# The rounded half of a gelu result copied by GpSimd instead of ScalarE, with a later due time for the half that follows

## The chip, the cores and the metric

The kernel runs on one core of a Trainium2 chip. A core has a matrix engine (TensorE, "PE" in the profile; its weight loads are shown apart as "PEld"), VectorE ("DVE"), ScalarE ("ACT"), GpSimd ("POOL") and SyncE ("SP"), which here only issues DMAs. Every engine works through its own list of instructions strictly in order, and waits for the others through semaphores. Operands lie in SBUF, results of matmuls in PSUM. The metric is the time of one execution on the device, in microseconds (us); less is better.

## What is computed

For 2048 rows x of width 512 the reference mixes two branches, a windowed attention with 32 heads of width 16 and a dense network with a gelu, by a sigmoid gate of each row:

```python
qkv = (x @ wqkv)                        # 32 heads of 16
scores = (q @ k.T) * 16 ** -0.5         # each row sees itself and the 255 rows before it
a = softmax(masked scores) @ v @ wo
h = gelu(x @ w1 + b1)                   # tanh form, width 1792
b = h @ w2 + b2
g = sigmoid((x * gate_w).sum(-1))
out = g * a + (1 - g) * b
```

Everything is float32. TensorE is given float32 numbers rounded to a shorter form ("fp32r"), so the kernel splits each operand of the dense products into a high half (the number rounded to fp32r) and a low half (the number minus its high half), and makes each product out of three matmuls: high by high, high by low, low by high.

## The kernel before

**Tiling.** Rows are worked in 4 blocks of 512. The dense work is one long stream: the qkv projection of the four blocks, then eight dense stages (four row blocks, each with the first and with the second half of the 1792 hidden columns), then the output projection. Each dense stage has a first part, "u", which makes 7 tiles of 128 hidden columns (12 matmuls each: 4 slices of the inner width, three matmuls each, lines 109 to 111), each followed by the gelu; and a second part, "y", which multiplies the 7 gelu results h with w2, for four groups of 128 rows.

**Attention runs in between.** While TensorE works through the dense stages, the main loop slips attention matmuls between the dense ones: line 522 makes a score tile of which VectorE takes row maxima (line 526); line 566 makes another score tile, of which ScalarE takes the exponential into a tile named pt (line 588); GpSimd zeroes the masked corners of pt (line 582, four instructions for a finished block) and copies the maxima into the operand of line 566 (line 548, "put", eight small copies per 512 rows); line 610 multiplies pt with v ("PV"). Each kind of score tile has three PSUM buffers. The last blocks of attention are masked by VectorE instead of GpSimd.

**Order.** The order of instructions on all engines is written out by the program. A counter in nanoseconds advances with each matmul that is issued; `after(ns, fn)` puts a piece of work into a heap with a due time, and it is appended to its engine's list when the counter passes that time. `need(key)` issues pending work until a key is done. So a due time is no wait: it only decides between which other instructions of its engine a piece of work stands. The waits come from data and from buffers being reused.

**The gelu** is function `gelu`, called 100 ns after the last matmul of a u tile. It has seven steps for each 128x512 tile: line 721 on ScalarE writes x1 = u + b1 into an SBUF buffer; f1 (line 724, ScalarE) squares u + b1 in PSUM; f2 (727, VectorE) forms the argument of tanh in sq; f3 (730, ScalarE) takes tanh; f4 (733, VectorE) makes x1 = (tanh + 1) * x1, which is twice the gelu; f5 (736) writes the high half h[:, 0], a copy that rounds to fp32r; f6 (739, VectorE) writes the low half h[:, 1] = x1 - h[:, 0] and marks h as issued. The tuple GELU holds the due times of f1 to f6 after the first step. The buffer tag "x1" has two buffers, so the line 721 of a tile waits until f6 of the tile two before it has read x1. Tag "sq" has two buffers as well, h has seven.

In part y the tiles of h are used in the order 0 to 5 for the first 128 rows, 0 to 2 for the second 128 rows, then tile 6 for the first rows (constant YSWAP = 3), and so on. Of the three matmuls of such a product the first two (lines 109 and 110) read the high half of h, and the third (line 111) reads the low half and waits for f6.

**Other work of the same engines** in the dense stages: weights are split like the activations, the high half by ScalarE (line 179), the low half by VectorE or, early on, in turn by GpSimd (line 183); line 631 (ScalarE) and 634 (VectorE) evacuate PV; line 814 (VectorE) evacuates y.

Of the kernel before, what the change touches and what calls it, by code (L numbers as in the profile page):

```python
# [12 lines left out]
AF = mybir.ActivationFunctionType  # L13
# [19 lines left out]
def gated_mix(ctx: ExitStack, tc: tile.TileContext, x, wqkv, wo, w1, b1, w2, b2, gate_w, out):  # L33
    nc = tc.nc
# [11 lines left out]
    def f32(ap):  # L46
        return ap.bitcast(F32)
# [68 lines left out]
    def after(ns, fn, *args):  # L116
        now[1] += 1
        heapq.heappush(todo, (now[0] + ns, now[1], fn, args))
# [598 lines left out]
    def gelu(p, f, h):  # L717

        x1 = sb.tile([128, T], F32, tag="x1", bufs=2, name=f"x1{h.name}")
        sq = sb.tile([128, T], F32, tag="sq", bufs=2, name=f"sq{h.name}")  # L720
        nc.scalar.activation(x1, p, AF.Identity, bias=b1c[:, f:f + 1])

        def f1():
            nc.scalar.activation(p, p, AF.Square, bias=b1c[:, f:f + 1])

        def f2():
            nc.vector.scalar_tensor_tensor(sq, p, GC, x1, op0=ALU.add, op1=ALU.mult)  # L727

        def f3():
            nc.scalar.activation(sq, sq, AF.Tanh, scale=GS)  # L730

        def f4():
            nc.vector.scalar_tensor_tensor(x1, sq, 1.0, x1, op0=ALU.add, op1=ALU.mult)

        def f5():
            nc.scalar.activation(h[:, 0], x1, AF.Copy)

        def f6():
            nc.vector.tensor_sub(h[:, 1], x1, f32(h[:, 0]))
            done.add(h.name)  # L740
        for ns, fn in zip(GELU, (f1, f2, f3, f4, f5, f6)):
            after(ns, fn)
# [258 lines left out]
START = 105000.0  # L1001
NORM = 6000
YSWAP = 3
GELU = (700, 1500, 3600, 4600, 6000, 7000)
XAT = 3
ORDER = 'mspf'
XOR = 1
# [38 lines left out]
```

## Time and profile before

| quantity | value |
|---|---|
| time, median of 3 runs (lowest, highest) | 742.09 us (740.79, 743.92) |
| time of the profiled execution | 741.31 us |
| its span, first to last instruction | 739.5 us |
| granted TensorE clock, share of full speed | 0.999 |
| VectorE busy | 516.3 us (70%) |
| ScalarE busy | 420.3 us (57%) |
| DMA queues' share of 16 engines, main queue | 82.6% |
| f6, line 739 (56 times) | 41.3 us, mean 738 ns |
| f4, line 733 (56 times) | 41.6 us, mean 743 ns |
| select, line 582 (538 times) | 217.7 us, mean 425 ns |

The profile is of one execution. A line such as "L736 ACT ACTIVATE h<-x1h" names the line of the kernel, the engine, the operation, and the tile written and read. A timeline row gives start and duration in us; where it ends in brackets, these hold the time that the engine sat idle before and what ended it. Matmuls are pipelined: a row of a matmul lasts about 0.39 us for 512 columns while the next one starts 0.23 us later, so that the starts tell the rate, and busy time of TensorE says little.

### The profile page before, as it was taken

The numbers are of one execution on the slowest core, as the hardware profiler recorded it, in microseconds if no ns is written. First come the engines' busy times: TensorE is split into PE (matmuls) and PEld (weight loads), VectorE is DVE, ScalarE is ACT, GpSimd is POOL, SyncE is SP. The second block draws the span as 40 slices with busy tenths as digits, with TensorE's granted clock in tenths as the row PEclk, the third lists the DMA queues.
The fourth block names the chain that finished last, engine by engine and source line by source line (L and its number), as shares of the span: only waits on it lengthen the run. The fifth ranks groups of instructions, "written<-read, shape, count | busy, mean of one in ns | idle before, by whom it ended". The sixth has DMA issues, their size and how long they took to land.

```text
span 739.5 us, 17486 instructions
## 1 busy us (share of the span) xinstructions
PE 729.2 (99%) x6129; PEld 603.7 (82%) x6129; DVE 516.3 (70%) x1567; ACT 420.3 (57%) x972; POOL 360.1 (49%) x846
## 2 busy tenths in 40 slices
PE   8999999999999999999999999999999999999998
PEld 7888888887788888888888887888888888877786
DVE  3632326789768867986798699767867886774552
ACT  4434532358537844863695479447735853795551
POOL 4200000339656765776587668757765775630000
PEclk9999999999999999999999999999999999999999
DMA  9989798999995687799676999996798799568672
GB/s 313 340 270 408 254 398 270 257 328 197 294 243 143 159 246 199 179 226 269 156 187 160 241 214 239 261 244 150 178 268 241 185 228 253 137 185 230 204 242 112
DMA packets 179255, 172.09 MB, mean 233 GB/s; under 512 B 56672, under 2 KB 122976, under 8 KB 179168
## 3 DMA queue, kind: packets, MB, share of 16 engines
q1 hardware_dynamic: 179168, 170.97, 82.6%
q8 instruction: 49, 0.80, 0.5%
q14 instruction: 38, 0.31, 0.2%
HBM read 108.53 MB, written 62.39 MB: 231 GB/s over the span
## 4 chain that ended last, share of the span: by engine, by line
PE 85%; DVE 5%; ACT 4%; DMA 4%; issue 2%; POOL 0%; SPq 0%; POOLq 0%; DVEq 0%; ACTq 0%
PE sm L522 9%; PE st L566 8%; PE pv_sm L610 7%; PE y L109 7%; PE y L111 7%; PE y L110 7%; PE u L109 5%; PE u L110 5%; PE u L111 5%; PE qk L109 4%; PE qk L111 4%; PE qk L110 4%; PE a L109 2%; PE v L109 2%; PE v L111 2%; PE v L110 2%
## 5 line engine op out<-in xcount | busy, mean ns | idle before, releaser
L526 DVE CUSTOM_DVE_ANT_0 sm<-sm,mask 128x320 f32<-128x320 f32 (+4 forms) x512 | 234.0, 484 | 87.1 <-PE sm L522 81.3
L588 ACT ACTIVATE pt<-st 128x320 f32<-128x320 f32 (+4 forms) x512 | 199.9, 426 | 138.1 <-PE st L566 135.0
L582 POOL TENSOR_SCALAR_AFFINE_SELECT pt<-pt 64x256 f32<-64x256 f32 (+1 forms) x538 | 217.7, 425 | 118.7 <-ACT pt L588 108.7
L522 PE MATMUL sm<-kd,qd 96*128 96x320 f32 (+4 forms) x512 | 152.9, 310 | 2.8 <-DVE M L526 2.7
L566 PE MATMUL st<-qs,ks 128*128 128x320 f32 (+4 forms) x512 | 153.7, 309 | 0.8 <-ACT pt L588 0.8
L548 POOL CAST qs<-tt 4x256 fp32r<-4x256 f32 x256 | 121.5, 475 | 47.7 <-DVE tt L541 33.3
L522 PEld LDWEIGHTS sm<-kd,qd 96*128 96x128 f32 x512 | 96.4, 188 | 26.1 <-DVE M L526 6.4
L566 PEld LDWEIGHTS st<-qs,ks 128*128 128x128 f32 x512 | 97.1, 190 | 18.1 <-ACT pt L588 2.2
L109 PE MATMUL y<-w,h 128*128 128x512 f32 x224 | 88.6, 396 | 0.6 <-DVE sqh L727 0.6
L111 PE MATMUL y<-w,h 128*128 128x512 f32 x224 | 87.9, 392 | 0.0
L110 PE MATMUL y<-w,h 128*128 128x512 f32 x224 | 87.8, 392 | 0.0
L109 PE MATMUL u<-mx,w 128*128 128x512 f32 x196 | 79.9, 408 | 0.0
L110 PE MATMUL u<-mx,w 128*128 128x512 f32 x196 | 77.3, 395 | 0.0
L111 PE MATMUL u<-mx,w 128*128 128x512 f32 x196 | 77.1, 393 | 0.0
L610 PE MATMUL pv_sm<-pt,vbuf 64*32 64x320 f32 (+4 forms) x1408 | 73.0, 346 | 0.0
L610 PE MATMUL pv_st<-pt,vbuf 64*32 64x320 f32 (+4 forms) x1408 | 72.6, 346 | 0.0
L526 DVE DVE_READ_ACCUMULATOR2_ANT M<- 128x1 f32 x512 | 71.6, 140 | 0.0
L610 PEld LDWEIGHTS pv_sm<-pt,vbuf 64*32 64x32 f32 x1408 | 48.9, 106 | 20.7 <-issue 1.7
L326 DVE TENSOR_TENSOR qke<-qk,qke 128x512 fp32r<-128x512 f32 x32 | 22.1, 689 | 46.2 <-ACT qke L323 30.4
L323 ACT ACTIVATE qke<-qk 128x512 fp32r<-128x512 f32 x32 | 19.1, 598 | 55.4 <-PE qk L111 32.9
L111 PEld LDWEIGHTS y<-w,h 128*128 128x128 f32 x224 | 42.0, 188 | 9.8
L109 PEld LDWEIGHTS y<-w,h 128*128 128x128 f32 x224 | 42.4, 189 | 4.5 <-DVE sqh L727 0.9
(148 smaller groups left out, 1288.6 us busy)
## 6 DMA issues: line engine op xcount, KB each, us to landing
kd<-SK SPq DMA_DIRECT2D x32, 384.0 KB
qs<-SQ SPq DMA_DIRECT2D x64, 192.0 KB
mx<-XT SPq DMA_DIRECT2D x24, 512.0 KB
SQ<-qke SPq DMA_DIRECT2D x16, 512.0 KB
SK<-qke SPq DMA_DIRECT2D x16, 512.0 KB
ND<-nd SPq DMA_DIRECT2D x32, 256.0 KB
raw_w<-in_B_w_dram SPq DMA_DIRECT2D x28, 256.0 KB
ks<-SK SPq DMA_DIRECT2D x32, 192.0 KB
```

What stands on the lines that cost most here:

```text
L109: nc.tensor.matmul(p, lh, rh, start=first, stop=False)
L110: nc.tensor.matmul(p, lh, rl, start=False, stop=False)
L111: nc.tensor.matmul(p, ll, rh, start=False, stop=last)
L323: nc.scalar.activation(e[:, h], p, AF.Copy)
L326: nc.vector.tensor_sub(e[:, 1 - h], p, f32(e[:, h]))
L522: nc.tensor.matmul(p[:, :w], qd[0:96, n, pr, 128 * j:128 * (j + 1)], kd[0:96, n, pr, k1 - w:k1], start=True, stop=True)
L526: nc.vector.tensor_tensor_reduce(p[:, :w], p[:, :w], mask[:, 320 - w:320], 1.0, -3e38, ALU.add, ALU.max, M[:, 2 * (b % RB) + hb, pr:pr + 1])
L548: nc.gpsimd.tensor_copy(dst, src.unsqueeze(1).broadcast_to([4, 2, RB, 32]))
L566: nc.tensor.matmul(p[:, :w], ks[:, slot(g_, kb // NB), pr, at:at + 128], qs[:, pr, k0:k0 + w], start=True, stop=True)
L582: nc.gpsimd.affine_select(out=v, in_=v, pattern=[[0, v.shape[1]], [1 - 2 * e, 64]], compare_op=ALU.is_ge, fill=0.0, base=-e, channel_multi ...
L588: nc.scalar.activation(pt[:, hf, pr, :w], p[:, :w], AF.Exp, scale=SCALE)
L610: nc.tensor.matmul(pv[r // 64][32 * i:32 * i + 32, q - c * T:e - c * T], vts[g_, b // NB][r:r + 64, v:v + 32], rhs(r), start=start, stop=s ...
```

## The change

The step f5 is issued to GpSimd as a copy (which rounds to fp32r by the type of its output), and f6 gets a due time of 8000 ns instead of 7000.

```diff
@@ gelu
         def f5():
-            nc.scalar.activation(h[:, 0], x1, AF.Copy)
+            nc.gpsimd.tensor_copy(h[:, 0], x1)
 
         def f6():
             nc.vector.tensor_sub(h[:, 1], x1, f32(h[:, 0]))
...
-GELU = (700, 1500, 3600, 4600, 6000, 7000)
+GELU = (700, 1500, 3600, 4600, 6000, 8000)
```

The due time of f5 itself stays at 6000 ns, and the number of instructions stays the same: 56 leave ScalarE's list and 56 come into GpSimd's.

## The prediction, made before the changed kernel was run

> **What bounds the kernel now.** I read the page's span and busy shares first, then the waits of the matrix engine, then the two operations that change places.
>
> ```profile
> span 739.5 us, 17486 instructions
> ...
> PE 729.2 (99%) x6129; PEld 603.7 (82%) x6129; DVE 516.3 (70%) x1567; ACT 420.3 (57%) x972; POOL 360.1 (49%) x846
> ```
>
> The profiled execution took 741.31 us, 1.8 us more than its span of 739.5 us, and stands 0.78 us below the median of 742.09 us. TensorE is busy 99% of the span, so a change to another engine can bring only what TensorE still waits. The table of waits (who waited for what, total us, times, longest) gives that:
>
> ```profile
> PEld sm L522 <- DVE M L526: 6.4, 12, 1.0
> ...
> PE sm L522 <- DVE M L526: 2.7, 6, 0.8
> ...
> PEld st L566 <- ACT pt L588: 2.2, 6, 0.8
> ...
> PE st L566 <- ACT pt L588: 0.8, 2, 0.5
> ```
>
> Waits for VectorE's row maxima come to 9.1 us, those for ScalarE's exponentials to 3.0 us: 12.1 us in all, at most, since the weight load and its matmul can both count one wait. So the most that relief of these two engines can bring is 12 us, 1.6%. On the other side there is no such limit: whatever makes TensorE late is paid in full.
>
> Where the dense part u runs, the helpers are close to full. Busy us of two stretches, the first u part and a later one:
>
> ```profile
> 160.00:190.00 30.00, 27.84 (x195) 21.72 (x194) 28.19 (x84) 25.03 (x56) 24.23 (x46) 1.00 0.94 246
> ...
> 290.00:322.00 32.00, 32.00 (x312) 26.97 (x312) 28.29 (x89) 26.08 (x58) 22.79 (x50) 1.00 0.73 169
> ```
>
> The columns are length, then PE, PEld, DVE, ACT and POOL. In the first, VectorE is busy 28.19 of 30 us (94%), ScalarE 83%, GpSimd 81%; TensorE stands still 2.16 us there and not at all in the second. The granted clock is 1.00 in both.
>
> **The change, operation by operation.** The groups by line give the prices (count, then total us and mean ns):
>
> ```profile
> L736 ACT ACTIVATE h<-x1h 128x512 fp32r<-128x512 f32 x56 | 36.0, 644 | 6.5 <-DVE x1h L733 6.5
> ...
> L195 POOL CAST qk<-raw_qk 128x512 fp32r<-128x512 f32 x1 | 0.6, 611 | 4.4 <-DMA raw_qk<-in_A_wqkv_dram 4.4
> ```
>
> ScalarE loses 56 copies of 644 ns, 36.0 us, and the 6.5 us in which it stood idle before them. GpSimd gets 56 copies. Line 195 is the same operation on the same shape, on GpSimd, at 611 ns: I take 0.61 us, though the burst of selects below took 8.14 / 16 = 0.51 us each and one of them 0.86, a sign that beside a busy VectorE it may be longer. GpSimd's load grows by 56 x 0.61 = 34 us; in a u part by 7 x 0.61 = 4.3 us, to about 90% of the first stretch above. No DMA is added or moved, and SP's queue stays as it was.
>
> The work itself is cheap on both engines. What counts is that each list is served in order. On ScalarE f5 stood between exponentials that were waiting for TensorE. On GpSimd it stands behind selects and puts, and f6 on VectorE, with all row maxima queued behind it, waits for it. In return f6 stands about 1 us further down VectorE's list: the program's clock advances 227 ns a dense matmul, and so do the starts in the trace, so 1000 ns of due time are 1 us.
>
> *Term 1, the first u part.* GpSimd, VectorE and ScalarE, in this order:
>
> ```profile
> 168.08 0.93 POOL L548 CAST qs<-tt 4x256 fp32r<-4x256 f32 x1
> ...
> 174.63 0.86 POOL L582 TENSOR_SCALAR_AFFINE_SELECT pt<-pt 64x256 f32<-64x256 f32 x1
> ```
>
> ```profile
> 172.54 8.14 POOL L582 TENSOR_SCALAR_AFFINE_SELECT pt<-pt 64x256 f32<-64x256 f32 x16
> ```
>
> ```profile
> 167.06 0.68 DVE L739 TENSOR_TENSOR h<-x1h,h 128x512 fp32r<-128x512 f32 x1
> ...
> 171.48 1.65 DVE L739 TENSOR_TENSOR h<-x1h,h 128x512 fp32r<-128x512 f32 x1
> ```
>
> ```profile
> 166.00 0.65 ACT L736 ACTIVATE h<-x1h 128x512 fp32r<-128x512 f32 x1
> ...
> 170.09 0.65 ACT L736 ACTIVATE h<-x1h 128x512 fp32r<-128x512 f32 x1
> ```
>
> GpSimd has a backlog here: the row of the 16 selects has no idle time in front of it, nor within it beyond 8.14 us of work. A select is queued 500 ns after the exponential that completes its block, f5 6000 ns after line 721. By that order the f5 that ScalarE did at 166.00 comes behind the put of 168.08, so its copy runs from 169.01 to 169.62; f6, which stood at 167.06 and would now stand at 168.06, waits 1.6 us. The f5 of 170.09 comes behind the select that ends at 174.63 + 0.86 = 175.49; with one copy already added to the backlog, it ends at 175.49 + 2 x 0.61 = 176.71, where f6 stood at 171.48 and would stand at 174.1 (1.0 for its due time, 1.6 for the wait before): 2.6 us more. VectorE thus holds its maxima back by 1.6 + 2.6 = 4.2 us. The first tile's f6 keeps its place and costs only its own 1 us on the x1 buffer, for which ScalarE's line 721 two tiles on has to wait. Against that, two removed f5 give ScalarE 1.2 us before that point. 4.2 - 1.2 = 3.0 us. Bounds: 0.5 (the backlog shrinks because exponentials come earlier) and 4.5 (nothing is given back).
>
> *Term 2, the start of part y.* There the last h tiles are needed soon after they are made. Row by row: f6 of a sixth tile and the matmul of line 111 that reads it; then GpSimd's last select ahead of the copy, f6, and the lines 109 and 111 of another sixth tile; then a third.
>
> ```profile
> 323.93 0.81 DVE L739 TENSOR_TENSOR h<-x1h,h 128x512 fp32r<-128x512 f32 x1
> ```
>
> ```profile
> 325.32 0.40 PE L111 MATMUL y<-w,h 128*128 128x512 f32 x1
> ```
>
> ```profile
> 391.72 0.86 POOL L582 TENSOR_SCALAR_AFFINE_SELECT pt<-pt 64x256 f32<-64x256 f32 x1
> ```
>
> ```profile
> 391.53 0.77 DVE L739 TENSOR_TENSOR h<-x1h,h 128x512 fp32r<-128x512 f32 x1
> ```
>
> ```profile
> 392.88 0.39 PE L109 MATMUL y<-w,h 128*128 128x512 f32 x1
> ...
> 393.35 0.39 PE L111 MATMUL y<-w,h 128*128 128x512 f32 x1
> ```
>
> ```profile
> 528.79 0.84 POOL L582 TENSOR_SCALAR_AFFINE_SELECT pt<-pt 64x128 f32<-64x128 f32 x1
> ```
>
> First place: f6 ends at 324.74, 1 us later at 325.74; the matmul stood at 325.32: 0.4 us lost. Second: the copy starts at 392.58, ends at 393.2, f6 (0.7 us) at 393.9; the matmul stood at 393.35: 0.55 us. Third: copy from 529.63 to 530.25, f6 to 530.95, its matmul stood at 530.91: nothing to speak of. The other stages have more room, by the same rows. Together 1.0 us; bounds 0 and 4 (0.5 in each of eight stages).
>
> *Term 3, PV.* TensorE's PV takes pt right after GpSimd's last select:
>
> ```profile
> 459.77 4.90 POOL L582 TENSOR_SCALAR_AFFINE_SELECT pt<-pt 64x256 f32<-64x256 f32 x12 [1.69 <-ACT pt L588]
> ```
>
> ```profile
> 464.77 0.24 PE L610 MATMUL pv_sm<-pt,vbuf 64*32 64x64 f32 x1
> ```
>
> The selects end at 464.67, PV starts 0.1 us later, and one copy falls inside the run of twelve: 0.61 - 0.1 = 0.5 us. Bounds 0 (selects come earlier, since the exponentials do) and 2.
>
> *Term 4, held maxima in the other six u parts with GpSimd.* A copy behind a burst makes f6 late by about 0.7 us in one or two tiles of each part, as at 391.72 (393.2 - 392.5). TensorE has three score buffers, a pair of maxima of room, so most is covered: I take 1.0 us, of about 5 us if nothing covers it.
>
> *Term 5, the gain.* ScalarE's exponentials come earlier by up to 0.6 us a tile. In the first u part this is in term 1. Elsewhere the waits for exponentials are 3.0 us at most, partly in the first part: I take 1.0 us back, bounds 0 and 6 (if waits for maxima go too).
>
> Sum: 3.0 + 1.0 + 0.5 + 1.0 - 1.0 = 4.5 us. On the profiled execution 741.31 + 4.5 = 745.8 us, on the median 746.6; I take 746.2 us.
>
> **The rivals.** *Covered after all.* The exponentials come earlier, so GpSimd's bursts start earlier and the copies meet no backlog; the extra 1 us of f6 hides them. For it: GpSimd idles 108.7 us in all waiting for exponentials. Against: in the rows above it has no idle time where the copies fall. Terms 1 to 4 at a quarter (1.4) less 1.0: 742 us.
>
> ```profile
> POOL pt L582 <- ACT pt L588: 108.7, 103, 2.8
> ...
> DVE h L739 <- ACT h L736: 1.5, 5, 0.4
> ```
>
> *Faster.* The waits behind maxima come from VectorE's f6 standing too early, ahead of maxima that were ready, and from f2 behind a crowded ScalarE. If f6 at 8000 ns lets the maxima by and f5's 36 us leave ScalarE, half of the 12 us goes while terms 1 to 4 cost 1 us: 742.09 - 6 + 1 = 737.1 us. It decides in the first u part: if GpSimd catches up before 168 us there, this or the former holds.
>
> *Engines in each other's way.* At 171.48 f6 took 1.65 us instead of 0.69; a GpSimd subtract was running from 171.29 to 172.58, and f6 ended 0.55 us behind that:
>
> ```profile
> 171.29 1.29 POOL L183 TENSOR_TENSOR w<-raw_w,w 128x512 fp32r<-128x512 f32 x1
> ```
>
> So VectorE and GpSimd hold each other up for whole instructions. If half of the 56 copies meet an f4, f6 or weight split of about 0.69 us, 28 x 0.69 = 19 us are lost on one of the two, and if a third of that reaches TensorE, 6 us come on top: 752 us. The Trainium skill says this in general: in SBUF — State Buffer, section "Who interferes with whom", a VectorE instruction with two SBUF inputs contends with a GpSimd instruction that reads SBUF, and the pair of ports is held for the whole instruction. The row of 171.48 agrees, and f4 and f6 are such instructions; the same rule holds for the selects of today, so how much more the copies add no row shows.
>
> **How the numbers follow.** Chances: the forecast (743 to 750) 0.50, covered 0.21, faster 0.11, in each other's way 0.18. A measurement of this kernel can tell about 0.5% (3.7 us) from no change: 738.4 to 745.8 counts as the same. Of the forecast's 0.50 a third lies below 745.8 (0.17). Slower 0.33 + 0.18 = 0.51; same 0.17 + 0.21 = 0.38; faster 0.11. The range leaves out the fastest case and the upper half of the last: 739.5 to 754.
>
> **What would show it.** Right: in the first u part f6 waits for GpSimd's copy by 1 us or more twice, and TensorE's time in 160 to 190 grows by 3 us; a wait of VectorE for line 736, now on GpSimd, of well over the 1.5 us that it has on ScalarE today; small stalls of line 111 at the start of y. Wrong: no wait of f6 for the copy, copies that start right behind f4, waits for exponentials and maxima under 6 us. If the copies last well over 0.61 us or f4 and f6 over 0.8 us, the last rival holds.

## The result, and the profile after

| | before | changed |
|---|---|---|
| median of 6 runs, us | 742.54 (740.79 to 743.92) | 751.80 (749.65 to 754.39) |
| ratio to before, 95% interval | 1 | 1.0124 [1.0102, 1.0146] |
| profiled execution, us; its span | 741.31; 739.5 | 753.85; 752.1 |

The changed kernel is slower by 1.24%, 9.2 us (0.0124 x 742.5). The forecast was slower, by 4.5 us, with 746.2 us as the time; the measured median lies inside the range of 739.5 to 754 and at twice the forecast loss.

The page of the changed kernel, the same two lines as before (busy us, share of the span, count):

```profile
span 752.1 us, 17486 instructions
...
PE 735.7 (98%) x6129; PEld 607.2 (81%) x6129; DVE 522.4 (69%) x1567; ACT 396.8 (53%) x916; POOL 393.9 (52%) x902
```

The move is there: 56 instructions fewer on ScalarE, 56 more on GpSimd, whose busy time grew by 33.8 us (360.1 to 393.9); 34 were reckoned. TensorE has the same 6129 matmuls, though they are shown busy for 6.5 us longer; some of this is two stretches at half clock, told of in the last section. The groups by line say that no instruction became dear:

```profile
L733 DVE SCALAR_TENSOR_TENSOR x1h<-sqh,x1h 128x512 f32<-128x512 f32 x56 | 43.5, 777 | 1.5 <-ACT sqh L730 1.5
...
L739 DVE TENSOR_TENSOR h<-x1h,h 128x512 fp32r<-128x512 f32 x56 | 40.9, 730 | 9.9 <-POOL h L736 9.6
...
L736 POOL CAST h<-x1h 128x512 fp32r<-128x512 f32 x56 | 34.5, 616 | 16.0 <-DVE x1h L733 13.1
```

The copy takes 616 ns on GpSimd (611 in the row of line 195), 644 on ScalarE before. f4 grew from 743 to 777 ns, f6 fell from 738 to 730. What grew is the idle time in front of them: f6 now waits 9.6 us for the copy, 1.5 us before.

Lines from the table of waits of the changed kernel (who waited for what: us in total, times, longest):

```profile
ACT x1h L721 <- DVE h L739: 16.8, 17, 2.3
...
POOL h L736 <- DVE x1h L733: 13.1, 7, 3.9
PEld sm L522 <- DVE M L526: 11.6, 20, 1.6
...
DVE h L739 <- POOL h L736: 9.6, 15, 1.4
...
PE sm L522 <- DVE M L526: 5.8, 9, 1.2
...
PEld st L566 <- ACT pt L588: 3.0, 4, 1.5
...
PE st L566 <- ACT pt L588: 2.4, 3, 1.1
```

Two things are to be seen. TensorE waits longer for both helpers: 17.4 us for VectorE's maxima (9.1 before) and 5.4 us for ScalarE's exponentials (3.0 before), although ScalarE has 36 us less to do. And the first row is one that I had not priced: ScalarE's line 721 waits 16.8 us in 17 tiles for f6, 2.6 us in 4 tiles before. The same row of the kernel before:

```profile
ACT x1h L721 <- DVE h L739: 2.6, 4, 1.3
```

GpSimd itself waits 13.1 us in 7 tiles for f4 before it can copy. The selects and puts behind those copies come later for it, but TensorE has only one short wait for GpSimd's work there (0.5 us, of PV for the selects).

The first u part is where the change could first bite. Busy times of the same two stretches (length, then PE, PEld, DVE, ACT, POOL, the granted clock):

```profile
160.00:190.00 30.00, 25.57 (x177) 20.14 (x176) 24.98 (x74) 21.11 (x47) 23.22 (x44) 0.94 0.86 221
290.00:322.00 32.00, 32.00 (x312) 26.88 (x310) 27.70 (x90) 21.47 (x50) 23.56 (x52) 1.00 0.72 184
```

TensorE stands still 4.4 us of the first 30 us, 2.2 before. VectorE did 25.0 us of work where it did 28.2. All three helpers do less in the same time: they wait for each other. Here are GpSimd, then VectorE, then ScalarE in that stretch of the changed kernel, and last ScalarE's line 721 before:

```profile
169.68 0.61 POOL L736 CAST h<-x1h 128x512 fp32r<-128x512 f32 x1
170.36 3.04 POOL L548 CAST qs<-tt 4x256 fp32r<-4x256 f32 x5
173.49 1.28 POOL L183 TENSOR_TENSOR w<-raw_w,w 128x512 fp32r<-128x512 f32 x1
174.72 2.06 POOL L582 TENSOR_SCALAR_AFFINE_SELECT pt<-pt 64x256 f32<-64x256 f32 x4
176.84 0.61 POOL L736 CAST h<-x1h 128x512 fp32r<-128x512 f32 x1
```

```profile
170.33 0.69 DVE L739 TENSOR_TENSOR h<-x1h,h 128x512 fp32r<-128x512 f32 x1 [1.08 <-POOL h L736]
...
177.49 0.86 DVE L739 TENSOR_TENSOR h<-x1h,h 128x512 fp32r<-128x512 f32 x1 [1.35 <-POOL h L736]
```

```profile
165.35 0.69 ACT L721 ACTIVATE x1h<-u,b1c 128x512 f32<-128x512 f32 x1 [2.29 <-DVE h L739]
...
171.06 0.69 ACT L721 ACTIVATE x1h<-u,b1c 128x512 f32<-128x512 f32 x1 [2.09 <-DVE h L739]
...
178.39 0.69 ACT L721 ACTIVATE x1h<-u,b1c 128x512 f32<-128x512 f32 x1 [2.33 <-DVE h L739]
```

```profile
163.69 0.69 ACT L721 ACTIVATE x1h<-u,b1c 128x512 f32<-128x512 f32 x1 [1.25 <-DVE h L739]
...
167.78 0.69 ACT L721 ACTIVATE x1h<-u,b1c 128x512 f32<-128x512 f32 x1
...
173.16 0.69 ACT L721 ACTIVATE x1h<-u,b1c 128x512 f32<-128x512 f32 x1 [0.41 <-DVE h L739]
```

The second copy (169.68) and the third (176.84) come after a put and after a block of selects, with puts, a subtract and these selects between them and no idle time, as forecast; f6 stands ready and waits 1.08 and 1.35 us. Each f6 that ends late is followed at once by a line 721 on ScalarE that waited 2 us for it, where the same three lines waited 1.25, 0 and 0.41 us before: the loss goes round a ring, x1 buffer to GpSimd to VectorE to x1 buffer.

### The profile page after: what moved, and what is told of

Its sections match the earlier page's. It is cut to its first block, busy times and chain, and to the rows that moved or that the text cites. A ratio compares the mean times of both kernels' runs of the same rounds, so it can differ in the third digit from the quotient of the medians.

```text
span 752.1 us, 17486 instructions
## 1 busy us (share of the span) xinstructions
PE 735.7 (98%) x6129; PEld 607.2 (81%) x6129; DVE 522.4 (69%) x1567; ACT 396.8 (53%) x916; POOL 393.9 (52%) x902
## 4 chain that ended last, share of the span: by engine, by line
PE 79%; POOL 8%; DVE 6%; DMA 3%; issue 2%; ACT 2%; SPq 0%; POOLq 0%; DVEq 0%; ACTq 0%
PE sm L522 8%; PE st L566 7%; PE pv_sm L610 6%; PE y L111 6%; PE y L109 6%; PE y L110 6%; POOL pt L582 5%; PE u L109 5%; PE u L110 4%; PE u L111 4%; PE qk L109 4%; PE qk L111 4%; PE qk L110 4%; PE a L109 2%; PE v L109 2%
## 5 line engine op out<-in xcount | busy, mean ns | idle before, releaser
L582 POOL TENSOR_SCALAR_AFFINE_SELECT pt<-pt 64x256 f32<-64x256 f32 (+1 forms) x538 | 219.9, 429 | 97.1 <-ACT pt L588 86.8
L111 PEld LDWEIGHTS y<-w,h 128*128 128x128 f32 x224 | 42.3, 189 | 11.5 <-DVE h L739 1.7
L339 POOL MEMSET vx<- 128x32 f32 x16 | 2.4, 156 | 89.2 <-DMA SK<-qke 30.5
L721 ACT ACTIVATE x1h<-u,b1c 128x512 f32<-128x512 f32 x56 | 38.4, 686 | 19.8 <-DVE h L739 16.8
```

The costliest lines, as they stand in the source:

```text
L111: nc.tensor.matmul(p, ll, rh, start=False, stop=last)
L582: nc.gpsimd.affine_select(out=v, in_=v, pattern=[[0, v.shape[1]], [1 - 2 * e, 64]], compare_op=ALU.is_ge, fill=0.0, base=-e, channel_multi ...
```

## The experiments

All are measured against the kernel before on the same chip. The theory: two prices, one for f6 waiting in GpSimd's list (VectorE's maxima are held), one for the later f6 (ScalarE waits for the x1 buffer). Its rivals: the later due time is free; VectorE and GpSimd merely hold each other up, or GpSimd is too full.

**Only the due time.** f5 stays on ScalarE.

```diff
-GELU = (700, 1500, 3600, 4600, 6000, 7000)
+GELU = (700, 1500, 3600, 4600, 6000, 8000)
```

> f5 stays on ScalarE; only the due time of f6 is 8000 ns. If the later due time carries the 9.2 us (f6 ends 1 us later, so ScalarE's line 721 two tiles on waits for the x1 buffer), the time is 747 to 752 us and the wait of line 721 for f6 rises from 2.6 us to 10 us or more. If f6 being held behind GpSimd's list carries it, the time stays within 2 us of before (741 to 745 us), and the wait is about 5 us.

Ratio 1.0060 [1.0042, 1.0079], +4.5 us: half of the loss, without GpSimd. Its waits:

```profile
ACT x1h L721 <- DVE h L739: 10.9, 16, 1.9
```

```profile
PEld st L566 <- ACT pt L588: 4.4, 7, 1.5
...
PE st L566 <- ACT pt L588: 3.0, 5, 1.1
```

TensorE's waits for exponentials rise from 3.0 to 7.4 us, those for maxima stay near (10.6 after 9.1). So at least part of the price of the due time is paid on ScalarE: line 721 waits, and the exponentials queued behind it come late; how large that part is, the runs with sq below tell. The time, 746.5 us, lies just under the 747 us that was expected of this theory; the other theory's 745 us is refuted less by the time than by the wait of 10.9 us. The first u part has little of this loss: from its first matmul to the first of part y it lasts 33.2 us in this run's profile and 32.7 us before.

**Only the engine.** f5 on GpSimd, f6 at 7000 ns.

```diff
-            nc.scalar.activation(h[:, 0], x1, AF.Copy)
+            nc.gpsimd.tensor_copy(h[:, 0], x1)
```

> f5 on GpSimd, f6 at 7000 ns as before. If f6 being held behind GpSimd's list carries the loss, f6 waits for the copy in more tiles, over 20 us in all instead of 9.6 us, and the time is that of the changed kernel or longer (751 to 757 us). If the later due time carries it, the time is near that of before (742 to 746 us).

Ratio 1.0228 [1.0208, 1.0248], +16.9 us, worse than the whole change and above the 757 us that was expected at most.

```profile
DVE h L739 <- POOL h L736: 29.9, 33, 2.2
...
PEld sm L522 <- DVE M L526: 19.7, 24, 2.5
```

f6 waits for the copy in 33 tiles. So the later due time does what it can do for f6: it takes 20 us off this wait (29.9 to 9.6). But it asks a price of its own, by another way. Some 4 us of this loss came up late in its profile, in the output projection (50.5 us from its first matmul to its last, 46.5 before), where one wait is 2.1 us long; that is not taken for part of the mechanism. Without them the loss would still be about 13 us.

**The changed kernel without the x1 wait.** f4 writes where the tanh stood, and f5 and f6 read it there; x1 is then free after f4.

```diff
-            nc.vector.scalar_tensor_tensor(x1, sq, 1.0, x1, op0=ALU.add, op1=ALU.mult)
+            nc.vector.scalar_tensor_tensor(sq, sq, 1.0, x1, op0=ALU.add, op1=ALU.mult)
...
-            nc.gpsimd.tensor_copy(h[:, 0], x1)
+            nc.gpsimd.tensor_copy(h[:, 0], sq)
...
-            nc.vector.tensor_sub(h[:, 1], x1, f32(h[:, 0]))
+            nc.vector.tensor_sub(h[:, 1], sq, f32(h[:, 0]))
```

> The changed kernel, but f4 writes its result into sq instead of x1, and f5 and f6 read it there: x1 is free after f4, and no ScalarE step waits for f6. If the loss reaches TensorE by way of ScalarE's wait for the x1 buffer (16.8 us in the changed kernel), the time falls to 743 to 747 us. If it comes from maxima held behind f6 on VectorE, it stays at 749 us or more, with VectorE's wait for the copy at about 10 us as now.

Ratio 1.0065 [1.0045, 1.0084], +4.8 us: 4.4 us of the 9.2 are gone, at the edge of what was expected. No wait of line 721 for f6 is left, and none of line 566 on TensorE for exponentials. VectorE's wait is nearly as it was, and so are TensorE's for maxima (15.5 us after 17.4):

```profile
DVE h L739 <- POOL h L736: 7.3, 13, 1.3
...
PE sm L522 <- DVE M L526: 4.9, 6, 2.1
```

The two prices thus come by two ways that can be told apart in the tables of waits: exponentials by way of ScalarE, which this run takes away, and maxima by way of VectorE, which it leaves. That the 4.8 us left are paid through the maxima is read from these waits; no run takes the maxima's way away alone.

**Load on GpSimd that nobody waits for.** The kernel before, with copies into a tile that is not used any more, two for each f5.

```diff
             nc.scalar.activation(h[:, 0], x1, AF.Copy)
+            for _ in range(2):
+                nc.gpsimd.tensor_copy(idle.rearrange("p (a b) -> p a b", b=64),
+                                      cut[:, 0].unsqueeze(1).broadcast_to([128, 5, 64]))
```

> The kernel before, with two GpSimd copies (128x320, from a small table into a tile that nobody reads) issued at each f5: GpSimd gets the added load, but nothing waits for it. If VectorE and GpSimd holding each other up, or selects that come later, carry the loss, the time rises by 3 us or more (745.5 us and up) and f4 and f6 take over 0.80 us on the mean. If f6 waiting for the copy and what follows from it carry it, the time stays within 2 us of before (741 to 744.5 us).

Ratio 1.0194 [1.0173, 1.0215], +14.4 us. I had not thought that load alone would cost that. The waits that are new are PV's for the selects (weight load and matmul count the same wait):

```profile
PEld pv_sm L610 <- POOL pt L582: 6.1, 7, 1.8
...
PE pv_sm L610 <- POOL pt L582: 4.6, 7, 1.4
...
PEld pv_st L610 <- POOL pt L582: 3.2, 4, 1.5
...
PE pv_st L610 <- POOL pt L582: 2.5, 3, 1.4
```

They come to 7.1 us on the matmuls and 9.3 us on the weight loads; for the rest of the 14.4 us I have no row. f4 takes 780 ns here and f6 747 ns, both under the 0.80 us that was named as the sign of the engines holding each other up. Two copies are 1.09 us for a tile (2 x 547 ns), 1.8 times the load of the change, so the run could not tell what 0.61 us costs. One copy can:

> The kernel before with one GpSimd copy a tile that nobody waits for (0.55 us, where the changed kernel's copy takes 0.61 us), instead of the two of the run before. If added load on GpSimd delays selects, and PV behind them, in proportion, the time is about half way, 748 to 751 us, with PV waiting for selects 2 us or more. If GpSimd has room for one copy but not for two, the time stays within 2 us of before (741 to 744.5 us) and PV waits for selects under 1 us.

Ratio 1.0011 [0.9997, 1.0026], +0.8 us, with 563 ns for a copy, near the 616 ns of the change, and one PV wait of 0.4 us in the profile (of the longest of its twelve executions, 747.58 us). GpSimd has room for one such copy a tile and not for two. That sets aside both the full GpSimd and the engines holding each other up as the cause of 9.2 us. In this run's profile a copy overlaps an f4 at least 5 times and an f6 at least 21 times; in that of the changed kernel, none of the 56 copies overlaps an f4 or an f6 and one overlaps a weight split on VectorE. The idle copy differs in two things: it is a little shorter, and it does not wait for f4.

**Where.** The change in the first u part alone, and in all but the first:

```diff
+        on_pool = n == 0
         def f5():
-            nc.gpsimd.tensor_copy(h[:, 0], x1)
+            if on_pool:
+                nc.gpsimd.tensor_copy(h[:, 0], x1)
+            else:
+                nc.scalar.activation(h[:, 0], x1, AF.Copy)
...
-        for ns, fn in zip(GELU, (f1, f2, f3, f4, f5, f6)):
+        for ns, fn in zip(GELU[:5] + ((8000,) if on_pool else (7000,)), (f1, f2, f3, f4, f5, f6)):
```

> The change in the first u part alone (7 tiles), the other 49 tiles as before. If the first u part carries the loss that its rows show (about 4 us, of which 1.7 us is one window of the clock at half), the time is 745 to 748 us. If it is made up later, 743 us or less.

> The change in the seven later u parts alone. If the loss adds up part by part (x1 buffer waits of ScalarE in most parts), the time is 746 to 749 us, and with the run of the first part alone the two losses add to about 9 us. If the first part sets all that follows, it is 744 us or less.

First part alone 1.0063 [1.0040, 1.0087], +4.7 us for 7 tiles; the rest (`n > 0`) 1.0076 [1.0058, 1.0093], +5.6 us for 49. Together 10.3 us, about the whole. The next run has f4 into sq in all parts, and engine and due time of the first part as before:

> f4 writes into sq; f5 on GpSimd and f6 at 8000 ns in the seven later u parts, the first u part as before. If the x1 buffer in the later parts and the first u part are the whole loss, the time is that of before within 2 us (740.5 to 744.5 us), and relief of ScalarE may show as a gain. If VectorE held behind GpSimd's copies costs much in the later parts too, it is 745 us or more.

Ratio 1.0019 [1.0006, 1.0033], +1.4 us. But f4 into sq helps the kernel before as well, to 0.9980, as the runs below show; against that base the change in the later parts costs 2.9 us, and 2.7 of the 5.6 us above are the buffer's. TensorE's waits for exponentials are down to 0.2 us, those for maxima up to 14.9 us (9.1 before). So even with the price of the buffer removed, the relief of ScalarE brings no gain: less waiting for exponentials stands against more waiting for maxima.

**The due time without the x1 wait, and sq alone.** f5 on ScalarE and f4 into sq, with f6 at 8000 and at 7000 ns:

> f5 on ScalarE, f6 at 8000 ns, and f4 writes into sq, so that line 721 doesn't wait for f6. If the x1 buffer is the whole of what the later due time costs (4.5 us alone), the time is that of before or less (739 to 743 us). If the later f6 costs in another way (part y waiting for the low half, maxima moved), it stays at 745 us or more.

> The kernel before, but f4 writes into sq, so that no step of ScalarE waits for f6 (2.6 us of such waits in the kernel before, 0.9 to 1.3 us of TensorE's waits behind them). If the x1 buffer costs the kernel before anything, the time is 0.5 to 2 us below before (740 to 742 us); if not, it is the same.

At 8000: 1.0018 [1.0001, 1.0035], +1.3 us, where it cost 4.5 us with x1; the median of 743.47 us is just above what was expected of the buffer as the whole price. At 7000: 0.9980 [0.9967, 0.9992], 740.40 us against 741.99: faster than the kernel before by about 1.5 us. All that it does is to let go of x1 after f4 instead of after f6.

| f5 on, f6 due | f5 and f6 read x1 | they read sq |
|---|---|---|
| ScalarE, 7000 | 1 (before) | 0.9980 |
| ScalarE, 8000 | 1.0060 | 1.0018 |
| GpSimd, 7000 | 1.0228 | not run |
| GpSimd, 8000 | 1.0124 (changed) | 1.0065 |

Read by rows: the buffer costs 1.5 us in the kernel before (0.0020 x 742), 3.1 us with the later due time, 4.4 us with the change. So 2.9 of the 9.2 us are what the change adds at the buffer (4.4 - 1.5). The other 6.3 us stay in the right column, from 0.9980 to 1.0065: 2.8 us come with the later due time (0.9980 to 1.0018), 3.5 us with the move to GpSimd (1.0018 to 1.0065). Each of these differences is uncertain by 1.5 to 2.5 us, by the intervals of its ratios. By what way the later f6 costs 2.8 us without the buffer is open; the profiles give a hint, TensorE's waits for maxima of 11.1 us at 8000 after 8.2 us at 7000.

## Why the prediction was wrong in size, and what of it held

**The step that failed** is the sentence on the due time: "In return f6 stands about 1 us further down VectorE's list". There the later due time is a return, taken as cover for f6. The x1 buffer is named once, for the first tile of the first part, and even that 1 us has no place in the sum (4.2 - 1.2 = 3.0); for all other tiles it was put at nothing. The cover is real (29.9 us of waiting became 9.6), but the due time alone costs 4.5 us, and part of that is charged to the x1 buffer. Rows of the kernel before show where there was no room. VectorE's f6, and ScalarE's lines 721 of the tile after it and of the tile that reuses its buffer:

```profile
442.03 0.92 DVE L739 TENSOR_TENSOR h<-x1h,h 128x512 fp32r<-128x512 f32 x1
```

```profile
437.70 0.68 ACT L721 ACTIVATE x1h<-u,b1c 128x512 f32<-128x512 f32 x1
...
442.98 0.69 ACT L721 ACTIVATE x1h<-u,b1c 128x512 f32<-128x512 f32 x1 [0.20 <-DVE h L739]
```

f6 ends at 442.95 and line 721 starts at 442.98. The wait shown is only 0.20 us, and this is why I passed it over: a short wait in a row tells how much is lost now, not how much room is left. With f6 later, such a tile pays nearly in full. In 17 of the 40 pairs of a tile and the one that reuses its buffer in the same part, the profile of before has less than 1 us from the end of f6 to the start of line 721, in 5 of them less than 0.1 us. What they lack to 1 us adds up to 10.7 us, an estimate from these rows; with the due time alone the wait of line 721 rose by 8.3 us (2.6 to 10.9). In the same part of the changed kernel:

```profile
446.31 0.69 ACT L721 ACTIVATE x1h<-u,b1c 128x512 f32<-128x512 f32 x1 [0.25 <-DVE h L739]
...
452.40 0.69 ACT L721 ACTIVATE x1h<-u,b1c 128x512 f32<-128x512 f32 x1 [0.94 <-DVE h L739]
...
457.99 0.69 ACT L721 ACTIVATE x1h<-u,b1c 128x512 f32<-128x512 f32 x1 [1.65 <-DVE h L739]
```

Priced by the run that has the due time alone, the missing term is 4.5 us, and 4.5 + 4.5 = 9.0 us would have been near the 9.2 measured. That the two add so well is partly luck: the engine alone costs 16.9 us, so they are not independent. Of the 4.5 us the table of the runs with sq gives 1.6 us to the x1 buffer (3.1 - 1.5) and leaves 2.8 us without a shown way. By place, the first part fell 1.7 us short of its term, and the later parts 4.1 us: terms 2 to 5 come to 1.5 us, 5.6 us was measured, and 2.7 us of it is the buffer.

**Term 1, the first u part**, forecast 3.0 us (0.5 to 4.5), measured 4.7 us [3.0, 6.5]. The mechanism was right, to the put and the select behind which the copies stand; the waits of f6 were 1.08 and 1.35 us, not 1.6 and 2.6, since VectorE's list was late itself by then. What I had wrong is the credit of 1.2 us for ScalarE: it was idle 2.29, 2.09 and 2.33 us in front of line 721 instead, 5 us more than before.

**Terms 2 and 3** hold in size. Part y waited for the low half 1.7 us in 4 places (forecast 1.0), by this row of the changed kernel:

```profile
PEld y L111 <- DVE h L739: 1.7, 4, 0.5
```

PV waited for selects once, 0.5 us by its weight load and 0.3 us by its matmul (forecast 0.5). The runs with idle copies show how close this one was: with a second copy PV waits at least 7.1 us for selects, and the loss is larger than that of the whole change.

**Terms 4 and 5** together were forecast at nothing (1.0 - 1.0). The later parts with the x1 wait taken out of them cost 1.4 us [0.4, 2.5] against before, but 2.9 us, uncertain by 1.4 us, against the kernel with sq alone. Terms 2 to 5 had 1.5 us for them, so at most little was missed here beside the buffer. The gain of term 5 did come on the side where it was looked for, waits for exponentials fell to 0.2 us in that run, but it went into waits for maxima.

**The rivals.** "Covered after all" and "faster" are refuted. "Engines in each other's way" named 752 us, which is what was measured, for a reason that the runs refute: with nearly the same load and nothing waiting for it the loss is 0.8 us, and its premise, that half of the copies meet an f4, f6 or weight split, came true for one copy of 56. The Trainium skill's page SBUF — State Buffer, section "Who interferes with whom", which this rival drew on, speaks of instructions that overlap in time; no copy of the changed kernel overlaps an f4 or an f6. The copy took 616 ns, and f4 and f6 stayed under the 0.8 us that was named as this rival's sign. f4 did become 34 ns longer (743 to 777), but that goes with the due time and not with the copies: it takes 768 ns with the due time alone and 747 ns with the engine alone. The forecast's chance of 0.51 for slower was cautious: it names its losses row by row, its gain only as a bound of 12.1 us of waits.

## What to carry to other kernels

Before a step is made later, look for the next user of each buffer that it reads, and measure the room from the end of the step to the start of that user: a wait of 0.2 us can mean that there is none. A move to an idler engine is judged by what stands ahead of it in that engine's list and by who waits for it, not by the engine's load: a copy of 0.56 us a tile cost 0.8 us with nobody waiting, and one of 0.62 us was part of 9.2 us with VectorE waiting. Where a buffer is in the way, another step may write into one that is free sooner: here that alone was worth 0.2%.

## What was not expected of the hardware

TensorE's granted clock fell to half for a whole stretch of 3.4 us, twice in the profiled execution of the changed kernel, behind stretches in which it had waited much. Four stretches of 3.4 us (the number after POOL's is the clock):

```profile
170.10:173.50 3.40, 1.67 (x8) 1.00 (x7) 2.62 (x6) 2.44 (x6) 3.08 (x7) 0.99 1.02 226
173.50:176.90 3.40, 3.40 (x10) 2.82 (x10) 2.64 (x10) 2.12 (x5) 3.29 (x6) 0.50 0.11 35
...
668.40:671.80 3.40, 2.03 (x9) 1.13 (x8) 2.45 (x5) 3.13 (x8) 0.75 (x1) 1.00 0.86 325
671.80:675.20 3.40, 3.40 (x10) 2.73 (x11) 1.94 (x5) 2.12 (x5) 0.12 (x1) 0.50 0.44 158
```

TensorE was busy 1.67 and 2.03 us of the 3.4 us ahead, and the half clock followed. TensorE: Matmul & The Clock Gate, a page of the Trainium skill, Part 1, states windows of 3413 ns after which the clock is halved when the window was idle; the length agrees, but here TensorE was idle for only 51% and 40% of the window ahead, and no single wait of TensorE ahead of 173.5 was longer than 1.2 us. What such a window costs stays open. Of the changed kernel's six runs the two with a mean clock of 0.995 took 753.85 and 754.39 us, the other four (0.997 and 0.998) 749.65 to 752.1 us; but with the change in the first part alone two runs at full clock took 746.27 and 746.26 us, and two at 0.998 took 745.20 and 744.56 us. With f4 into sq the shortest run had 0.995 (745.80 us) and the longest 1.000 (749.55 us). So the stalls come first, and the half clock is not needed to explain the loss: the runs at full clock lose 3.8 us with the change in the first part alone (two runs) and 5.1 us with it in the later parts alone (three runs), against the median of before.
